# Loading x of the next block in eight transfers, each behind its own weight fetch, in a linear-attention and gated feed-forward kernel

## The chip, the core and the metric

One core of a Trainium2 chip runs the whole program. The metric is the device time of one execution in microseconds (us). Five engines work side by side, each through its own queue in order: TensorE (PE in the profile, its weight loads PEld), VectorE (DVE), ScalarE (ACT), GpSimd (POOL) and SyncE (SP), which issues nearly all transfers (DMAs) here. An instruction that waits holds up everything behind it in its engine's queue.

## The reference

Linear attention over 8 batches, 8 heads, 576 tokens and a head width of 64, followed by a feed-forward stage in which two products are multiplied element by element:

```python
def phi(x):
    proj = np.einsum('bhsd,df->bhsf', x, w_phi)
    proj = proj - np.max(np.abs(proj), axis=-1, keepdims=True)
    return np.concatenate([np.exp(proj), np.exp(-proj)], axis=-1)
q_p, k_p = (phi(q), phi(k))
kv = np.einsum('bhsf,bhsd->bhfd', k_p, v)
z = np.sum(k_p, axis=2)
num = np.einsum('bhsf,bhfd->bhsd', q_p, kv)
den = np.einsum('bhsf,bhf->bhs', q_p, z)[..., None] + 1e-06
attn = num / den                      # 8 x 8 x 576 x 64
x = attn.transpose(0, 2, 1, 3)        # 4608 tokens x 512
a = x @ w_a                           # 512 x 1536
b = x @ w_b
out = (a * b) @ w_out                 # 1536 x 512
```

The weights of the second stage are 64-bit floats, which the kernel decodes itself. All products are made in single precision out of two parts: each operand is split into a high part that TensorE takes and the low remainder, and three matmuls (high by high, low by high, high by low) stand for one.

## The kernel before

**The two passes.** The attention leaves x, normalised, in device memory, one buffer `xnorm[b]` for each batch of 576 tokens. The feed-forward stage runs over its 1536 inner columns in two halves. The first pass makes the first 768 columns, in blocks of 384 tokens, between the steps of the attention, and leaves its partial result in `part`. The second pass (`second_pass`, L803) makes the other 768 columns in six blocks of 768 tokens and adds `part`. This is the stretch from about 804.6 us to the end.

**A block of the second pass.** It works on three "quads" q = 0, 1, 2, each two columns of 128 wide, by Winograd's form of a 2 by 2 block product with seven factors: w11, w12, s2, s1, s3, w22, s4. One product (`product`, L721) multiplies one factor of the weights a and b by the same factor of x, in 12 matmuls of 128 by 128 by 384 columns: 21 products, 252 matmuls in a block. `evict` copies a product from PSUM with ScalarE, `add` adds the next one with VectorE, and `hi` and `lo` split the results h. The products with the output weights (L843, 126 matmuls in a block) follow, partly between those of the third quad.

**The streamed weights.** The factors of a and b lie in device memory (`kept`). Every product ends with `feed()` (L1016), which fetches (`fetch`, L566) the factor of the fourth product after it, 512 KB, into the slot that the product has just set free; a ring of four slots. So a fetch waits at the head of SyncE's queue until its product's matmuls are done, and has to land before the fourth product after it. Counted through a block, the feeds are: 1 to 5 for quad 0 (w11 to s3), 6 and 7 for quad 1 (w11, w12), 8 and 9 for quad 0 (w22, s4), 10 to 12 for quad 1 (s2, s1, s3), 13 and 14 for quad 2 (w11, w12), 15 and 16 for quad 1 (w22, s4), 17 and 18 for quad 2 (s2, s1), 19 to 21 for the rest of quad 2.

**x of the next block.** `factors_of_x(j + 1)` (L658) is a generator that `second_pass` moves on between its own steps. It fills two tiles `x32` of 128 partitions by 2 halves by 768 tokens, c = 0 and c = 1. A block of 768 tokens always spans two batches, so each tile takes two loads, and each load brings both halves i = 0 and 1 of the model's 512 rows for one run of tokens. After the four loads come the factors of x: for each factor and c a cast to the high part by ScalarE and a subtraction by VectorE (L156 and L163 in `split`), with four more subtractions for each c (L690 to L693).

**The order.** The kernel's instructions are put into the engines' queues by a planner, which goes by the program's order as priority and by its own estimate of when each operand is ready. `behind(feeds, ...)` (L392) ties a transfer's place in SyncE's queue to a place after the last fetch that has been made so far. The four loads of a block are tied to feeds 9, 11, 12 and 14. The three first loads of `part` (`given_load`, L817) are tied to feed 16. For the first block (j = 0) the loads are issued without such a tie, at the end of the first pass; there the tiles `x32` are shared with the decoding of the weights.

Of the kernel before, what the change touches and what calls it, by code (L numbers as in the profile page):

```python
# [3 lines left out]

# [14 lines left out]
P = 128  # L19
# [43 lines left out]
def tile_kernel(ctx, tc, qP, qD, km, kr, vm, vr, w_phi, w_two, eye, w_a, w_b, w_out, out):  # L63
# [13 lines left out]
    nc = tc.nc  # L77
    B, H, _, S = qD.shape
# [23 lines left out]
    xnorm = [dpool.tile([DM, S], F32, name=f"xnorm{b}") for b in range(B)]  # L102
# [57 lines left out]
    def split(hi, lo, src, eng_hi, eng_lo):  # L160

        copy(eng_hi, hi, src)
        eng_lo.tensor_tensor(lo, src, hi, op=ALU.subtract)  # L163
# [228 lines left out]
    def behind(what, issue):  # L392

        with tc.issue_after(what[-1].ins):
            issue()
# [170 lines left out]
    def fetch(key, place, name):  # L566
        t = place[0].tile([P, 2, 2, DM // 2], F32R, tag=place[1], name=f"back_{name}")
        feeds.append(nc.sync.dma_start(t.bitcast(F32), kept[key]))
        weights[key] = t
# [88 lines left out]
    def factors_of_x(j, pool, xs):  # L658


        n = T2 // 2
        half = NCC // 2
        x = [None] * NCC
        for c in range(half):
            x32 = pool.tile([P, 2, T2], F32, tag="x32", bufs=2, name=f"x32_1_{j}_{c}")
            x[c], x[c + half] = x32[:, 0], x32[:, 1]
            t = j * T2
            while t < (j + 1) * T2:
                b, s0 = divmod(t, S)
                m, t0 = min(S - s0, (j + 1) * T2 - t), t - j * T2  # L670
                rows = xnorm[b].rearrange("(i c p) s -> p c i s", i=2, p=P)[:, c, :, s0 : s0 + m]
                load = lambda: (nc.sync if j else nc.sync).dma_start(x32[:, :, t0 : t0 + m], rows)
                behind(feeds, load) if j else load()
                t += m
                yield

        def factor(c, k, src):
            hl = [pool.tile([P, n], F32R, tag=f"x{k}{part}", bufs=half, name=f"x{k}{part}_1_{j}_{c}") for part in "hl"]
            split(*hl, src, nc.scalar, nc.vector)
            xs[c][k] = hl  # L680

        for k, i in (("w11", 0), ("w12", half)):
            for c in range(half):
                factor(c, k, x[c + i][:, :n])
                yield
        for c in range(half):
            (x11, x12), (x21, x22) = ((t[:, :n], t[:, n:]) for t in (x[c], x[c + half]))
            sums = pool.tile([P, 2, n], F32, tag="xs", name=f"xs_1_{j}_{c}")
            t1, t2, t3, t4 = sums[:, 0], sums[:, 1], x12, x21
            nc.vector.tensor_tensor(t1, x12, x11, op=ALU.subtract)  # L690
            nc.vector.tensor_tensor(t2, x22, t1, op=ALU.subtract)
            nc.vector.tensor_tensor(t3, x22, x12, op=ALU.subtract)
            nc.vector.tensor_tensor(t4, x21, t2, op=ALU.subtract)  # L693
            yield
            factor(c, "s2", t2)
            factor(c, "s1", t1)
            yield
            factor(c, "s3", t3)
            factor(c, "w22", t4)
            yield  # L700
        for c in range(half):
            factor(c, "s4", x[c + half][:, n:])
            yield
# [3 lines left out]
    def in_turn(issue, wanted):  # L707
        with tc.issue_after(issued[0].ins) if issued[0] and wanted else nullcontext():
            issued[0] = issue()

    def winograd(q, xs, hs, u, spaces, feed):


# [7 lines left out]
        def product(k, to):  # L721
            start = to not in acc
            if start:
                opened(to)
            for i, nm in enumerate("ab"):
                w = weight(q, nm, k)
                for c in range(NCC // 2):
                    xh, xl = xs[c][k]
                    cols = slice(c * P, (c + 1) * P)
                    for n_, (w_, x_) in enumerate(((w[:, 0, cols], xh), (w[:, 0, cols], xl), (w[:, 1, cols], xh))):  # L730
                        at = dict(start=(start and c == n_ == 0), stop=(c > 0 and n_ == 2))
                        in_turn(lambda: nc.tensor.matmul(acc[to][i], w_, x_, skip_group_check=True, **at), u.startswith("1_0"))  # L732
            feed()
# [67 lines left out]
        yield  # L801

    def second_pass(xs, spaces, feed):  # L803
        n = T2 // 2
        pool = pools_moe[-1]
        nq = NFS[1] // 2
        for j in range(NT // T2):
            src, dst = (t.rearrange("(c p) s -> p c s", p=P)[:, :, j * T2 : (j + 1) * T2] for t in (part, out))
            hs = [{} for _ in range(nq)]
            x_next = factors_of_x(j + 1, spaces["x"], xs) if (j + 1) * T2 < NT else iter(())  # L810
            quads = [winograd(q, xs, hs[q], f"1_{j}_{q}", spaces, feed) for q in range(nq)]
            acc, given, us = {}, {}, []
# [107 lines left out]
    def run(work, steps=None):  # L920

        while work and steps != 0:
            if next(work[0], work) is work:
                work.popleft()
            elif steps is not None:
                steps -= 1
# [8 lines left out]
    def home(f, nm):  # L935
        return wpool, f"w_{f}_{nm}"

    kept, begun, feeds = {}, set(), []
    weights, pools_moe, xpools, block_x, blocks, marks, loads = {}, [ps_moe], [xpool], {}, [0], [], []
    with ExitStack() as c:  # L940
        pools = attention_pools(c)
# [39 lines left out]
    with ExitStack() as c:  # L981
        pool = c.enter_context(tc.tile_pool(name="stage", bufs=1))
        stage = stage_second(xin, pool)
        ahead = itertools.chain(
            *(load_factors(q, nm, stage, own, pool) for q in range(nq) for nm in "ab"),
            factors_of_x(0, xin, xs),
        )
        last = work.pop()
        due = 0.0
        while work:  # L990
            run(work, 1)
            due += AHEAD
            while due >= 1:
                next(ahead, None)
                due -= 1
        for _ in ahead:
            pass
        next(last)
        outs = deque(pair for pair in pairs if pair[0] == "o")
        places = deque()  # L1000
        for f in range(NFS[0]):
            next(last)
            for nm in "ab":
                if outs:
                    own[outs.popleft()] = home(f, nm)
                else:
                    places.append(home(f, nm))
            if f % 2:
                for _ in load_factors(f // 2, "o", stage, own, pool):
                    pass  # L1010
# [5 lines left out]
    def feed():  # L1016

        used[0] += 1
        if used[0] > FIRST and order:
            key = order.popleft()  # L1020
            fetch(key, ring[0], "_".join(map(str, (used[0], *key))))
            ring.rotate(-1)

    run(deque([last]))
    places.extend(home(f, "o") for f in range(NFS[0]))
# [67 lines left out]
```

## Time and profile before

| | |
|---|---|
| runs | 1215.03, 1215.25 and 1224.24 us, median 1215.25 us |
| profiled execution | 1216.38 us, with a span of 1214.6 us from first to last instruction |
| granted TensorE clock | 0.999 of full speed over the span |
| PE busy | 1180.6 us, 97% |
| DVE busy | 972.5 us, 80% |
| ACT busy | 778.3 us, 64% |
| device memory traffic | 225.14 MB, mean 185 GB/s |

A row of the profile names the line of the kernel, the engine, the operation, the tile written and the tiles read ("pa<-xw11h,back_w": the product of a, from the high part of x's factor w11 and a fetched weight tile). In brackets stands how long the engine was idle before the instruction and what released it. PE's busy time includes pipelined overlap, so its lost time shows better at the weight loads, of which one stands before each matmul.

### The profile page before, as it was taken

The page shows a single profiled execution, that of the slowest core. Times are in us where ns is not written, and L with a number is a line of the kernel's source. Part 1 is how long each engine was busy: PE and PEld are TensorE (multiplying, and loading weights), DVE is VectorE, ACT ScalarE, POOL GpSimd, SP SyncE. Part 2 cuts the span into 40 slices and gives each one's busy share as a digit, 9 for nine tenths or more (in the row PEclk, how much of TensorE's full clock was granted, in tenths as well). Part 3 has the DMA queues.
Part 4 walks back from the last instruction along what each step waited for, and adds up shares of the span by engine and source line. Part 5 has one row for each costly group of instructions (what it writes and reads, how often), then busy time and mean ns, then how long its engine had stood idle before and what let it go on. Part 6 is the DMA issues. An engine that isn't in the chain of part 4 may idle for free.

```text
span 1214.6 us, 20190 instructions
## 1 busy us (share of the span) xinstructions
PE 1180.6 (97%) x7086; PEld 1124.5 (93%) x7086; DVE 972.5 (80%) x1733; ACT 778.3 (64%) x1656; POOL 152.4 (13%) x69
## 2 busy tenths in 40 slices
PE   8889999999999999999999999999999999999998
PEld 5567788999999999999999999999999999999997
DVE  6967888988898989898888478977768596868665
ACT  5767788878888878888788445644435353535332
POOL 2322222121221121131122000000000000000000
PEclk9999999999999999999999999999999999999999
DMA  8766764554455454545342578759586776768572
GB/s 234 225 213 183 190 185 120 151 157 124 143 146 152 129 155 114 160 128 174 109 132 55 161 241 296 258 161 317 170 270 214 224 249 216 258 202 298 169 245 86
DMA packets 146166, 225.14 MB, mean 185 GB/s; under 512 B 40912, under 2 KB 87760, under 8 KB 146064
## 3 DMA queue, kind: packets, MB, share of 16 engines
q1 hardware_dynamic: 145616, 223.58, 60.7%
q8 instruction: 56, 0.92, 0.3%
q14 instruction: 46, 0.38, 0.1%
q10 hardware_dynamic: 448, 0.26, 0.1%
HBM read 174.74 MB, written 49.05 MB: 184 GB/s over the span
## 4 chain that ended last, share of the span: by engine, by line
PE 58%; DVE 18%; DMA 14%; ACT 5%; issue 3%; SPq 1%; DVEq 0%; ACTq 0%
PE po L843 9%; PE pa L732 8%; PE pb L732 8%; PE pa L619 6%; PE po L642 6%; PE pb L619 6%; PE kvps L304 6%; PE pn L386 5%; DMA x<-xnorm 3%; PE pq L362 2%; PE pk L247 1%; DMA part<-o 1%; DVE qs L168 1%; DMA rec<-r 1%; DMA raw_a<-in_w_a 1%
## 5 line engine op out<-in xcount | busy, mean ns | idle before, releaser
L366 POOL PARTITION_ALL_REDUCE mb<-p x64 | 152.1, 2377 | 523.3 <-ACT p L363 441.9
L619 PE MATMUL pa<-xh,w_a 128*128 128x384 f32 x576 | 166.2, 341 | 2.4 <-ACT kvh L329 1.2
L619 PE MATMUL pb<-xh,w_b 128*128 128x384 f32 x576 | 161.4, 338 | 0.0
L642 PE MATMUL po<-hh,w_o 128*128 128x384 f32 x576 | 153.0, 338 | 1.8 <-ACT hh L156 1.2
L619 PEld LDWEIGHTS pa<-xh,w_a 128*128 128x128 f32 x576 | 105.3, 188 | 4.2 <-ACT kvh L329 1.6
L642 PEld LDWEIGHTS po<-hh,w_o 128*128 128x128 f32 x576 | 104.0, 188 | 3.1 <-ACT hh L156 1.5
L619 PEld LDWEIGHTS pb<-xh,w_b 128*128 128x128 f32 x576 | 104.8, 188 | 0.5
L642 PE MATMUL po<-hl,w_o 128*128 128x384 f32 x288 | 96.7, 338 | 1.1 <-DVE hl L163 1.1
L619 PE MATMUL pa<-xl,w_a 128*128 128x384 f32 x288 | 97.7, 339 | 0.0
L619 PE MATMUL pb<-xl,w_b 128*128 128x384 f32 x288 | 96.7, 336 | 0.0
L163 DVE TENSOR_TENSOR qel<-qe,qeh 128x1152 fp32r<-128x1152 f32 x46 | 62.3, 1354 | 30.0 <-ACT qeh L156 26.6
L843 PE MATMUL po<-hh_s,own_o 128*128 128x384 f32 x288 | 80.3, 336 | 0.7 <-ACT u L831 0.5
L168 DVE TENSOR_TENSOR qs<-q,qs 64x576 fp32r<-64x576 f32 x52 | 64.1, 1232 | 14.6 <-ACT qs L156 13.4
L843 PE MATMUL po<-hh_w,own_o 128*128 128x384 f32 x216 | 59.1, 334 | 0.0
L387 ACT COPY xn<-pn 65x288 f32<-65x288 f32 x128 | 49.1, 396 | 15.3 <-PE pn L386 12.9
L261 ACT ACTIVATE ke<-kd 128x512 f32<-128x512 f32 x64 | 40.8, 638 | 24.5 <-DVE kd L253 22.3
L642 PEld LDWEIGHTS po<-hl,w_o 128*128 128x128 f32 x288 | 54.1, 188 | 1.9 <-DVE hl L163 1.7
L156 ACT CAST qeh<-qe 128x1152 fp32r<-128x1152 f32 x46 | 53.4, 1161 | 2.3 <-PE pn L386 2.2
L370 ACT ACTIVATE qe<-p 128x576 f32<-128x576 f32 x64 | 44.6, 696 | 15.7 <-DVE qel L163 10.5
L843 PEld LDWEIGHTS po<-hh_s,own_o 128*128 128x128 f32 x288 | 52.6, 188 | 2.0 <-ACT u L831 1.2
L619 PEld LDWEIGHTS pa<-xl,w_a 128*128 128x128 f32 x288 | 54.2, 188 | 0.3
L619 PEld LDWEIGHTS pb<-xl,w_b 128*128 128x128 f32 x288 | 54.1, 188 | 0.1
(302 smaller groups left out, 3421.4 us busy)
## 6 DMA issues: line engine op xcount, KB each, us to landing
back_s<-kept_s SPq DMA_DIRECT2D x71, 512.0 KB
back_w<-kept_w SPq DMA_DIRECT2D x52, 512.0 KB
q<-in_qD SPq DMA_DIRECT2D x52, 288.0 KB
k<-in_km SPq DMA_DIRECT2D x55, 256.0 KB
xun<-xn SPq DMA_DIRECT2D x64, 144.0 KB
x<-xun SPq DMA_DIRECT2D x32, 288.0 KB
rb<-rec SPq DMA_DIRECT2D x32, 288.0 KB
xnorm<-x SPq DMA_DIRECT2D x32, 288.0 KB
```

The lines of the kernel that those rows point to most:

```text
L156: eng.copy(dst, src)
L163: eng_lo.tensor_tensor(lo, src, hi, op=ALU.subtract)
L168: eng_lo.tensor_tensor(hi_lo[D:], src[D:], hi_lo[D:], op=ALU.subtract)
L304: nc.tensor.matmul(st["kv_ps", b, pr][:width, j], v_[:, j, :width], e_[:, j], start=(left == NFULL and j == 0 and n_ == 0), stop=(left == ...
L366: nc.gpsimd.partition_all_reduce(mb, p32, P, bass_isa.ReduceOp.absmax)
L370: nc.scalar.activation(e[:, 0], p32, AF.Exp)
L386: nc.tensor.matmul(pn[: D + 1, :HALF], kv_[:, 2 * j + s, :], e_[:, s, tok], **at)
L387: nc.scalar.copy(xn[: D + 1, tok], pn[: D + 1, :HALF])
L619: nc.tensor.matmul(acc, w[:, cc * P : (cc + 1) * P], x, start=(k == 0), stop=(k == 3 * NCC - 1))
L642: nc.tensor.matmul(accs[cc], w[:, cc * P : (cc + 1) * P], h, **at)
L732: in_turn(lambda: nc.tensor.matmul(acc[to][i], w_, x_, skip_group_check=True, **at), u.startswith("1_0"))
L843: in_turn(lambda: nc.tensor.matmul(acc[m, to], w_, h_, skip_group_check=True, **f), False)
```

## The change

`factors_of_x` makes two loads out of each: one for i = 0 and one for i = 1, so eight loads of half the size (288, 192 or 96 KB for 576, 384 or 192 KB). All eight are made when the generator is first moved on; for j > 0 they are not issued there but put into a queue, `between`. `feed()` takes one of them off after each fetch and places it behind that fetch. The generator still gives way four times before the factors, so its later steps fall where they fell; whatever is left in the queue by then is issued at once. The first move comes after feed 9, so the eight loads stand behind feeds 10 to 17. For j = 0 all eight are issued at the first step, with no tie.

```diff
+from functools import partial
...
                 m, t0 = min(S - s0, (j + 1) * T2 - t), t - j * T2
-                rows = xnorm[b].rearrange("(i c p) s -> p c i s", i=2, p=P)[:, c, :, s0 : s0 + m]
-                load = lambda: (nc.sync if j else nc.sync).dma_start(x32[:, :, t0 : t0 + m], rows)
-                behind(feeds, load) if j else load()
+                for i in range(2):
+                    rows = xnorm[b].rearrange("(i c p) s -> p c i s", i=2, p=P)[:, c, i, s0 : s0 + m]
+                    load = partial(nc.sync.dma_start, x32[:, i, t0 : t0 + m], rows)
+                    between.append(load) if j else load()
                 t += m
-                yield
+        for _ in range(4):
+            yield
+        while between:
+            behind(feeds, between.popleft())
...
-    kept, begun, feeds = {}, set(), []
+    kept, begun, feeds, between = {}, set(), [], deque()
...
             fetch(key, ring[0], "_".join(map(str, (used[0], *key))))
             ring.rotate(-1)
+            if between:
+                behind(feeds, between.popleft())
```

## Rows read from the trace of the kernel before

**Rows 1.** The page's first part, busy time and share of the span by engine.

```profile
PE 1180.6 (97%) x7086; PEld 1124.5 (93%) x7086; DVE 972.5 (80%) x1733; ACT 778.3 (64%) x1656; POOL 152.4 (13%) x69
```

**Rows 2.** Busy time in one stretch, the first five blocks of the second pass. Columns: the stretch and its length, PE, PEld, DVE, ACT and POOL busy with instruction counts, granted clock, DMA share, GB/s.

```profile
804.60:1141.00 336.40, 330.47 (x1887) 326.77 (x1888) 249.37 (x502) 145.05 (x318) 0.00 (x0) 1.00 0.72 234
```

**Rows 3.** The chain of work that ended last, in order of time: start, length, what. One run of six matmuls without a stall.

```profile
971.80 1.04 PE pa L732 x6
```

**Rows 4.** Who waited for whom from 804 to 1193 us: who, for what, us in total, times, longest. Weight loads (PEld) only.

```profile
PEld pa L732 <- ACT top L740: 5.0, 7, 1.3
PEld pa L732 <- ACT hh_w L748: 1.9, 1, 1.9
PEld pa L732 <- ACT low L740: 1.6, 2, 0.8
...
PEld pb L732 <- ACT low L740: 1.1, 1, 1.1
```

**Rows 5.** The timeline of PE and of its weight loads at single waits: start, length, engine, line, what, and in brackets the idle time before it and its releaser.

```profile
916.84 0.19 PEld L732 LDWEIGHTS pa<-xs3h,back_s 128*128 128x128 f32 x1 [0.31 <-ACT top L740]
...
965.29 0.41 PE L732 MATMUL pa<-xw11h,back_w 128*128 128x384 f32 x1 [1.65 <-DMA back_w<-kept_w]
...
1097.56 0.19 PEld L732 LDWEIGHTS pa<-xw11h,back_w 128*128 128x128 f32 x1 [0.73 <-ACT top L740]
...
1117.87 0.19 PEld L732 LDWEIGHTS pa<-xs3h,back_s 128*128 128x128 f32 x1 [0.57 <-ACT top L740]
...
1165.30 0.19 PEld L732 LDWEIGHTS pa<-xw11h,back_w 128*128 128x128 f32 x1 [0.96 <-ACT top L740]
```

**Rows 6.** SyncE's timeline in the third block of the pass (with one load of the second block ahead): start, time until the last issue of the row ended, what, count. Here the fetch of feed 9 is at 959.51, feeds 10 and 11 at 961.59, 13 and 12 (the planner has them in this order) at 967.67, 14 at 971.83, 15 and 17 at 973.91, 16 at 978.07.

```profile
901.77 0.43 SPq L672 DMA_DIRECT2D x<-xnorm  x1
...
959.51 0.32 SPq L568 DMA_DIRECT2D back_w<-kept_w  x1
959.93 0.39 SPq L672 DMA_DIRECT2D x<-xnorm  x1
961.59 2.40 SPq L568 DMA_DIRECT2D back_w<-kept_w  x2
964.05 0.44 SPq L672 DMA_DIRECT2D x<-xnorm  x1
967.67 2.40 SPq L568 DMA_DIRECT2D back_s<-kept_s  x2
970.13 0.43 SPq L672 DMA_DIRECT2D x<-xnorm  x1
971.83 0.32 SPq L568 DMA_DIRECT2D back_s<-kept_s  x1
972.21 0.43 SPq L672 DMA_DIRECT2D x<-xnorm  x1
973.91 2.40 SPq L568 DMA_DIRECT2D back_s<-kept_s  x2
978.07 0.32 SPq L568 DMA_DIRECT2D back_w<-kept_w  x1
978.44 2.63 SPq L821 DMA_DIRECT2D o<-part  x3
```

**Rows 7.** The chain that ended last, in order of time: single transfers from their issue to the release of what waited for them. The first is a load of x, the second a fetch of 512 KB, the third a store of 192 KB, the fourth a load of 384 KB.

```profile
896.10 6.97 DMA x<-xnorm
...
959.51 5.65 DMA back_w<-kept_w
...
1198.85 1.94 DMA out_x<-o
...
1200.84 3.50 DMA o<-part
```

**Rows 8.** ScalarE's timeline in the second block (first two rows) and the third.

```profile
903.15 0.51 ACT L156 CAST xw11h<-x 128x384 fp32r<-128x384 f32 x1 [3.51 <-DMA x<-xnorm]
903.57 0.47 ACT L740 COPY low<-pb 128x384 f32<-128x384 f32 x1
...
976.67 0.51 ACT L156 CAST xw11h<-x 128x384 fp32r<-128x384 f32 x1 [2.90 <-DMA x<-xnorm]
```

**Rows 9.** Busy time by stretch in the third block; columns as in rows 2.

```profile
974.00:979.00 5.00, 5.00 (x31) 5.00 (x30) 3.29 (x8) 2.17 (x5) 0.00 (x0) 1.00 1.01 368
...
984.00:989.00 5.00, 5.00 (x31) 5.00 (x30) 5.00 (x12) 4.29 (x11) 0.00 (x0) 1.00 0.58 197
989.00:994.00 5.00, 5.00 (x30) 5.00 (x29) 5.00 (x12) 3.29 (x8) 0.00 (x0) 1.00 0.48 152
...
999.00:1007.00 8.00, 8.00 (x48) 8.00 (x47) 5.49 (x12) 4.09 (x9) 0.00 (x0) 1.00 0.66 191
```

**Rows 10.** The timelines of PE and VectorE: the first matmul of the block after, which reads the new x, and the first subtraction on the tile c = 1.

```profile
993.48 0.33 PE L732 MATMUL pa<-xw11h,back_w 128*128 128x384 f32 x1
...
977.22 0.56 DVE L163 TENSOR_TENSOR xw11l<-x,xw11h 128x384 fp32r<-128x384 f32 x1 [1.71 <-ACT xw11h L156]
```

**Rows 11.** SyncE's own waits over the second pass, and one issue of a transfer of 128 rows (a store) in its timeline.

```profile
SPq L568 <- PE pb L732: 198.5, 100, 9.6
...
874.08 0.34 SPq L828 DMA_DIRECT2D out_x<-o  x1
```

**Rows 12.** Busy time in the stretch between the attention's end and the second pass; columns as in rows 2.

```profile
757.00:804.60 47.60, 46.42 (x268) 46.09 (x266) 46.53 (x111) 29.95 (x72) 0.00 (x0) 1.00 0.69 226
```

## The prediction

> **What bounds the kernel now.** I read the page's first part, then the busy time of the five blocks that load a next x, then the waits of TensorE's weight loads, and last the queues around the x loads. TensorE is busy 97% of the span [rows 1], so only a stall of TensorE can be won. How much there is to win comes from a count. A block has 252 + 126 = 378 matmuls, and an undisturbed run takes 1.04 us for six [rows 3], so a block without a stall takes 65.5 us and five take 327.6. They took 336.4 [rows 2]: 8.8 us are lost in five blocks, 0.7% of the whole time. That is the ceiling of anything done to x's loads in this pass.
>
> Where the lost time sits: the weight loads waited 5.0 us for ScalarE's evictions "top", 2.7 us for "low" (1.6 and 1.1), and 1.9 us for what the view calls a cast [rows 4]. That last one is really a fetch: the matmul at 965.29 was released by the landing of `back_w` after 1.65 us [rows 5], and the fetch, of feed 9, took 5.65 us from its issue to that release [rows 7]. The waits for "low" of 1.1 us stand behind x: at 903.15 ScalarE had sat 3.51 us before a cast of x, and the eviction comes right behind it in the same queue [rows 8].
>
> **The change, part by part.**
>
> *The load behind feed 9 goes.* Now an x load is issued 0.4 us after that fetch (959.93 after 959.51), and the product that needs the fetch would have started at 965.29 - 1.65 = 963.64, 4.1 us after its issue [rows 5, 6]. The first part will stand behind feed 10, so this fetch runs with nothing of x after it for two more microseconds. The wait cannot fall to zero: the last block loads no x, and there the same place waits 0.96 us for "top" [rows 5]. What is late next is thus that eviction. Of the third block's wait of 1.9 us [rows 4] I count 1.9 - 0.5 = 1.4 gained, of the fifth block's 0.73 [rows 5] 0.2, with 0.5 as the remainder, between nothing and the 0.96. Sum: 1.6 us gained. Ends: no gain, and 1.9 + 0.7 = 2.6.
>
> *x arrives later.* The first tile (c = 0) is complete now with the second load. Afterwards its last part stands behind feed 12, which the planner has put after 13: in the second block that is the place of the load at 901.77 [rows 6]. A load of x took 976.67 - 972.21 = 4.5 us [rows 6, 8] to 7.0 us [rows 7] to the release of its cast, so c = 0 would be ready at about 906.3 to 908.8 instead of 903.1, that is 3.1 to 5.6 us later. The second tile's last part moves behind feeds 16 and 17, to about 978.4 from 972.21, 6.2 us later [rows 6]. Its landing then lies near 983, still 10 us before the first matmul that reads it at 993.48 [rows 10]. Two subtractions on it (0.56 us each, the first at 977.22 [rows 10]) move into a stretch where VectorE is full, 5.00 of 5.00 us at 984 and at 989; after 999 it has 2.5 us free out of 8 [rows 9]. Price between 0 and 1.1 us a block, 5.5 in all; I take 0, because PE has no idle time in those rows and the new x has the 10 us.
>
> *Where ScalarE then waits.* The casts of x stand among the evictions of quads 1 and 2, and the planner places them by its own estimate of the landing. If the casts move back with the loads, the stall of 1.1 us at 904 goes and those of 0.31 and 0.57 us for "top" and 1.6 us for "low" [rows 4, 5], at the evictions of quad 2, may grow, since more of x's work now falls beside them. Ends: all of these gone, -(1.1 + 0.3 + 0.6 + 1.6) = -3.6 us; or the casts stay ahead of the evictions, and the 3.1 us is paid in each of five blocks, +15.5. I take 0: the planner knows that the parts are tied to later fetches, and moves their casts; what it does not know, the landing under load, it has wrong by as much now as then.
>
> *More transfers, the same bytes.* Four more issues a block, 0.34 us each by the store of 128 rows, are 1.4 us of SyncE; it waits 198.5 us for PE in front of fetches [rows 11]. That wait is the cover. Without it each part would hold the next fetch by 0.3 us. I take 0. The load rate flattens: x is spread over eight products where it stood in six. In the densest row the DMA engines were busy throughout, at 368 GB/s [rows 9], so the bytes that move out of such a stretch free it, but what waits on fetches there has slack: PE runs 5.00 of 5.00.
>
> *The first block.* Its eight loads are issued up to three steps earlier in the program's order, with no tie. PE loses 1.2 of 47.6 us there [rows 12], so nothing large is to be won; four issues more are 1.4 us of SyncE ahead of weight loads that PE's work covers. I take 0, with ends -0.5 and +1.4.
>
> **Sum.** 1216.38 us for the profiled execution, less 1.6, is 1214.8. That execution stands 1.1 above the median of the runs shown, 1215.25, so on the median's scale: 1213.6 us.
>
> **A rule that speaks against it.** A 192 KB store took 1.94 us and a 384 KB load 3.50 [rows 7], so 192 KB more cost 1.56 us; of the smaller transfer 1.94 - 1.56 = 0.38 us is then a fixed part, an estimate across two kinds of transfer. The Trainium skill (DMA: Bandwidth & Descriptors, Rules for kernel authors) says to merge small transfers into one large one and names 1 MiB for full bandwidth, which would forbid the halving. The rows agree in sign, not in weight, for the parts here. By the rule the time would be that of the third rival; by the rows it is the sum above.
>
> **Rivals.**
> 1. *All of x's stalls go*: fetch 9 at its full gain (2.6) and the evictions' 3.6 us give 1215.25 - 6.2 = 1209.0; with every loss of these blocks gone, 8.8, 1206.4. For it: the DMA engines are full exactly where x comes. Against it: the place after feed 9 waits for "top" in the block without x too.
> 2. *ScalarE's queue holds an eviction behind a later x* (slower). Place: the copy "low" behind the cast of c = 0 [rows 8]. Price: 3.1 us in each block where the planner leaves the cast ahead of the copy. It decides from the point where c = 0 lands later than the copy could run. In two blocks it gives 1213.6 + 6.2 = 1219.8, in all five 1229.1. For it: x is later by design, and ScalarE has waited 3.51 us for this landing already [rows 8]. Against it: the planned place moves too.
> 3. *Each transfer has its fixed price in a full queue*: four times 0.38 is 1.5 us of delay a block for fetches at feeds 10 to 17. If no slack took it up, 7.6 us in five blocks, 1222.9. Against it: those fetches have four products' time, some 8 us, before they are needed.
> 4. *The change does nothing*: the planner puts the parts into the same order of landing, or gains and losses cancel: 1215.3.
>
> **How the numbers follow.** Chances: forecast 0.58, its own range 1210.5 to 1217; rival 1 0.13; rival 2 0.16, a third of it in all blocks; rival 3 0.04; rival 4 0.09. About 1% is what a measurement of this kernel can tell from no change: below 1203.1 or above 1227.4. No case reaches 1203; I leave 0.02 for a new order by the planner that nobody asked for. Slower by over 1% is the hard form of rival 2 with something for rival 3 and for a bad order: 0.07. The rest, 0.91, is within 1%. The range leaves out the hard form of rival 2 and the ends: from 1207.5, between rival 1's two values, to 1221, over rival 2's soft form.
>
> **What would show it.** Right: x loads of the later pass alternate with fetches, 40 instead of 20, each of 288, 192 or 96 KB; the wait of the third block's first w11 product of quad 2 falls from 1.9 to about 0.5 us with "top" as its releaser; the five blocks together take 333 to 336 us. For rival 1 they take 330 or less, with hardly a PE wait for "low". For rival 2 ScalarE sits longer in front of `xw11h` and PE right behind it for "low". For rival 3 the fetches of feeds 10 to 17 take longer from issue to release, and PE waits for `back_s`. My forecast is wrong if the five blocks change by more than 6 us, or if the first pass or its end, before 804.6 us, moves by more than 2 us.

## The result, and the profile after

The changed kernel took 1236.43 us in the median of six executions (1229.49 to 1237.91), the kernel before 1217.97 us beside them: a ratio of 1.0121, with a 95% interval of 1.0091 to 1.0151. (Every ratio here is an estimate from all executions of both kernels; the two medians alone would give 1.0152.) The prediction had 1213.6 us, no higher than 1221, and 91% on a change of less than 1%.

The profiled execution of after took 1229.49 us, the shortest of the six, with a span of 1227.7 us; it is 13.1 us above the one of before, so the loss in this trace is smaller than that of the medians, 18.5 us. The first part of its page, to be held against [rows 1]:

```profile
PE 1184.6 (96%) x7086; PEld 1127.0 (92%) x7086; DVE 973.5 (79%) x1733; ACT 779.9 (64%) x1656; POOL 152.8 (12%) x69
```

The counts are the same: no engine has more to do, yet PE is busy 4.0 us longer and idle for the other 9.1. Windows tell where. First the second pass of the kernel before, from its first matmul (columns as in rows 2):

```profile
804.65:1214.00 409.35, 398.17 (x2268) 392.57 (x2268) 291.88 (x583) 166.31 (x363) 0.00 (x0) 1.00 0.68 222
```

Then the same matmuls of after, and below them its first five blocks (1887 matmuls, as in [rows 2]) and three short stretches:

```profile
806.97:1154.40 347.43, 335.06 (x1887) 329.44 (x1888) 250.29 (x502) 146.07 (x318) 0.00 (x0) 0.99 0.70 227
806.97:1227.00 420.03, 402.82 (x2268) 395.34 (x2268) 292.85 (x583) 167.35 (x363) 0.00 (x0) 0.99 0.67 216
808.30:811.50 3.20, 3.20 (x12) 3.20 (x12) 2.52 (x7) 1.42 (x4) 0.00 (x0) 0.50 0.82 294
922.60:925.80 3.20, 2.37 (x12) 2.05 (x12) 3.20 (x8) 2.56 (x7) 0.00 (x0) 1.00 0.12 47
1060.80:1064.00 3.20, 3.20 (x10) 3.20 (x11) 3.19 (x7) 1.18 (x4) 0.00 (x0) 0.51 0.24 95
```

The pass begins 2.3 us later and takes 10.7 us more. The prediction had allowed 2 us for that start, but the 2.3 need not come from the change: two kernels further down (e6, e12) have the instructions of before in the same order on every engine up to here, and their passes begin at 808.21 and 799.78. Of the 10.7 us, 6.0 are idle time of PE (420.03 - 402.82 = 17.2 for 409.35 - 398.17 = 11.2), and for 4.7 PE is busy longer. Two stretches of 3.2 us at about half the granted clock account for some 3.2 of these. The loss lies in the five blocks that load a next x, which took 347.4 us for 336.4; the prediction had called itself wrong from a change of 6 us on. Who waited for whom in the second pass of after, from 804 to 1206 us (columns as in [rows 4]):

```profile
ACT xw12h L157 <- DMA x<-xnorm: 14.7, 7, 3.9
ACT xw11h L157 <- DMA x<-xnorm: 12.7, 8, 3.6
PEld pa L737 <- ACT top L745: 12.6, 9, 3.1
...
PEld pa L737 <- ACT low L745: 3.9, 4, 1.3
```

And in the same view of before, ScalarE's wait for x:

```profile
ACT xw11h L156 <- DMA x<-xnorm: 13.3, 7, 3.5
```

ScalarE waits 27.4 us for x where it waited 13.3, and PE's weight loads wait 12.6 us for "top", for 5.0 before [rows 4]. The timeline of PE at the longest of these waits, and that of PE or its weight loads at the two places where before had waited for a fetch:

```profile
922.60 0.44 PE L737 MATMUL pa<-xs3h,back_s 128*128 128x384 f32 x1 [2.56 <-ACT top L745]
...
970.42 0.19 PEld L737 LDWEIGHTS pa<-xw11h,back_w 128*128 128x128 f32 x1 [0.84 <-ACT top L745]
970.45 0.41 PE L737 MATMUL pa<-xw11h,back_w 128*128 128x384 f32 x1 [0.55 <-ACT top L745]
...
991.26 0.44 PE L737 MATMUL pa<-xs3h,back_s 128*128 128x384 f32 x1 [0.80 <-ACT top L745]
...
1060.75 0.59 PE L737 MATMUL pa<-xs3h,back_s 128*128 128x384 f32 x1 [2.76 <-ACT top L745]
...
1109.04 0.19 PEld L737 LDWEIGHTS pa<-xw11h,back_w 128*128 128x128 f32 x1 [0.53 <-ACT top L745]
...
1130.78 0.44 PE L737 MATMUL pa<-xs3h,back_s 128*128 128x384 f32 x1 [1.71 <-ACT top L745]
```

The rows at 970.4 and 1109.04 are the third and fifth block's first product of quad 2: the predicted gain came (1.65 us for a fetch in [rows 5] became 0.55 for "top"). The other four rows are one place, the product s3 of quad 2, in four of the five blocks. In before the weight load at the same place waited 0.31 us in the second block and 0.57 in the fifth [rows 5]. What stands behind it is told by the chain of waits in the second block (start, length, what):

```profile
914.19 6.21 DMA x<-xnorm
...
920.42 0.51 ACT xw11h L157
920.94 0.15 ACT hh_s L753
...
921.25 0.51 ACT xs1h L157
921.76 0.41 ACT hh_s L753
922.17 0.38 ACT top L745
...
922.60 1.32 PE pa L737 x6
```

Read from the bottom: PE waits for the eviction "top", which stands in ScalarE's queue behind two splits `hh_s` of quad 1 and casts of x, and the first of those casts waits for the last part of x, issued at 914.19. In the third, fourth and fifth block the chain to the same place also passes through VectorE, where a subtraction on x (L695) stands ahead of quad 1's last step (L796); the clearest case of that stands under e2.

ScalarE's timeline in the second block of after has the waits in brackets:

```profile
911.70 0.51 ACT L157 CAST xw11h<-x 128x384 fp32r<-128x384 f32 x1 [1.05 <-DMA x<-xnorm]
...
916.78 0.51 ACT L157 CAST xw12h<-x 128x384 fp32r<-128x384 f32 x1 [1.63 <-DMA x<-xnorm]
...
918.15 0.51 ACT L753 CAST hh_s<-top 128x384 fp32r<-128x384 f32 x1 [0.45 <-DVE top L792]
920.42 0.51 ACT L157 CAST xw11h<-x 128x384 fp32r<-128x384 f32 x1 [1.76 <-DMA x<-xnorm]
920.84 0.51 ACT L753 CAST hh_s<-low 128x384 fp32r<-128x384 f32 x1
...
922.08 0.47 ACT L745 COPY top<-pa 128x384 f32<-128x384 f32 x1
```

In before the casts of the second tile stood just as much ahead of quad 1's splits, and x was there in time:

```profile
910.29 0.51 ACT L156 CAST xw11h<-x 128x384 fp32r<-128x384 f32 x1 [1.33 <-DMA x<-xnorm]
910.71 0.51 ACT L156 CAST xw12h<-x 128x384 fp32r<-128x384 f32 x1
...
913.55 0.52 ACT L748 CAST hh_s<-top 128x384 fp32r<-128x384 f32 x1 [0.67 <-DVE top L787]
...
916.31 0.47 ACT L740 COPY top<-pa 128x384 f32<-128x384 f32 x1
```

The loads moved back; the casts of the second tile hardly did: of them only `xw11h` moved, behind one of three splits. Those of the first tile did move: in this block they now stand, from 908.05 on, behind quad 1's copy "low" at 905.41, as the prediction had it, and the wait of 1.1 us for that copy [rows 4, 8] is gone.

How late x is shows in the cast `xw11h` of each tile, which in both kernels starts when x lands: 911.70 for 903.15 [rows 8] with c = 0, 920.42 for 910.29 with c = 1. The block itself is 4.0 us later by then, as VectorE's first addition of "low" shows, in before and in after:

```profile
899.67 0.56 DVE L744 TENSOR_TENSOR low<-pa,low 128x384 f32<-128x384 f32 x1 [2.43 <-ACT low L740]
```

```profile
903.67 0.56 DVE L749 TENSOR_TENSOR low<-pa,low 128x384 f32<-128x384 f32 x1 [2.46 <-ACT low L745]
```

Against its own block, x is 8.5 - 4.0 = 4.5 us later with c = 0 and 10.1 - 4.0 = 6.1 with c = 1.

### The profile page after: what moved, and what is told of

It is laid out like the page before. It is cut to its first block, busy times and chain, and to the rows that moved or that the text cites. A ratio compares the mean times of both kernels' runs of the same rounds, so it can differ in the third digit from the quotient of the medians.

```text
span 1227.7 us, 20239 instructions
## 1 busy us (share of the span) xinstructions
PE 1184.6 (96%) x7086; PEld 1127.0 (92%) x7086; DVE 973.5 (79%) x1733; ACT 779.9 (64%) x1656; POOL 152.8 (12%) x69
## 4 chain that ended last, share of the span: by engine, by line
PE 52%; DVE 19%; DMA 16%; ACT 7%; issue 4%; SPq 1%; DVEq 0%; ACTq 0%
PE pa L737 9%; PE pb L737 9%; PE po L848 8%; PE pa L620 6%; PE pb L620 6%; DMA x<-xnorm 5%; PE kvps L305 5%; PE po L643 4%; PE pn L387 4%; DMA rec<-r 2%; DVE qs L169 2%; PE pq L363 1%; DMA rb<-rec 1%; DMA raw_a<-in_w_a 1%; PE pk L248 1%
```

## The experiments

Two theories stood at the start. **A**: the places of the loads cost, because x lands later and ScalarE's queue, with the casts of x in it, holds the evictions. **B** (rival 3): the number of transfers costs. A ratio is to the kernel before, run beside it on the same chip, with its 95% interval.

**Eight halves at the old places (e1).** Against before, each load is cut in two, still behind feeds 9, 11, 12 and 14:

```diff
-                load = lambda: (nc.sync if j else nc.sync).dma_start(x32[:, :, t0 : t0 + m], rows)
-                behind(feeds, load) if j else load()
+                for i in range(2):
...
+                    load = partial(nc.sync.dma_start, x32[:, i, t0 : t0 + m], rows)
+                    behind(feeds, load) if j else load()
```

> Edit: the eight half loads of the change, but two of them behind each of the fetches where the four whole loads stood (feeds 9, 11, 12, 14); the first block's loads halved too, two at each step. Theory A (the later places of the parts are what costs: the casts of tile c = 1 wait in ScalarE's queue ahead of the casts and the eviction 'top' that quad 2's s3 product needs): ratio to before 0.997 to 1.004, PE's waits for 'top' back to about 5 us. Theory B (eight transfers of half the size cost more than four): ratio 1.009 to 1.013, as the change itself. Theory C (the first block's loads at the first step, and the slower start after 804 us that follows, cost the time): ratio 1.000 to 1.004, with the start of the pass as before.

1.0005 [0.9990, 1.0020]. Eight transfers for four, and four more issues a block, cost nothing that can be measured here (the weight loads' wait for "top" is 6.3 us, for 5.0 in before). B falls. The Trainium skill (DMA: Bandwidth & Descriptors, Rules for kernel authors) says to join small transfers into large ones; for parts of 288, 192 and 96 KB beside this much other traffic the run shows no price.

**Four whole loads at late places (e2).** Against before, uncut, behind feeds 11, 13, 15 and 17:

```diff
-                behind(feeds, load) if j else load()
+                between.extend((None, load)) if j else load()
...
+            load = between.popleft() if between else None
+            if load:
+                behind(feeds, load)
```

> Edit: four whole loads as before, but late: behind feeds 11, 13, 15 and 17, so that each tile is complete where the change completes it; the first block as before. Theory A: ratio to before 1.007 to 1.014, ScalarE waits 2 to 4 us per block for x in front of the casts of quad 1's h, and PE waits 2 to 3 us at quad 2's s3 for 'top'. Theory B: 0.998 to 1.003. Theory C: 0.998 to 1.003.

1.0116 [1.0082, 1.0149]: the whole loss without any halving. Two waits of its second pass, and PE's timeline at the longest of them, in the fourth block, show the same place as after:

```profile
ACT xw11h L157 <- DMA x<-xnorm: 25.4, 10, 4.3
PEld pa L737 <- ACT top L745: 11.8, 10, 4.4
```

```profile
1060.80 0.69 PE L737 MATMUL pa<-xs3h,back_s 128*128 128x384 f32 x1 [4.09 <-ACT top L745]
```

But here the chain of waits that leads to it goes through VectorE:

```profile
1047.75 5.77 DMA x<-xnorm
...
1053.64 0.56 DVE xs L695
...
1057.95 0.47 DVE x L698
1058.42 0.47 DVE low L793
...
1059.36 0.48 DVE low L796
...
1059.86 0.51 ACT hh_s L753
1060.37 0.39 ACT top L745
```

From the landing of x on, VectorE worked without a pause. Eight of its instructions (L695 to L698 and four subtractions of `split`), at 0.47 us each 3.8 us in all, are for the next x and stand in its queue ahead of L796, the step that quad 1's last split needs, and "top" stands behind that split in ScalarE's queue. So theory A holds with VectorE's queue beside ScalarE's.

**The change without its part for the first block (e3).** The loads for j = 0 go back to four, one at each step:

```diff
-                    between.append(load) if j else load()
+                if j:
...
+                else:
+                    rows = xnorm[b].rearrange("(i c p) s -> p c i s", i=2, p=P)[:, c, :, s0 : s0 + m]
+                    nc.sync.dma_start(x32[:, :, t0 : t0 + m], rows)
```

> Edit: the change, with the first block's four loads whole and one at each step as before. Theory A: ratio to before 1.008 to 1.012; the wait at the start of the pass goes back from 2.5 to about 1.4 us and its stretch at the lower clock goes, 2 to 3 us in all. Theory B: 1.010 to 1.013. Theory C: 0.998 to 1.004.

1.0096 [1.0062, 1.0129]. The five blocks carry at least most of the loss; whether the first block's loads carry the remaining 0.25% is not told apart, since the two intervals overlap. The traces leave little for them: PE's wait at the first matmul of the pass is 1.1 to 2.0 us in the kernels with the first block's loads of before (nine profiles, this one at 1.1), and 2.0 to 2.7 us in the four that issue all eight at the first step.

**The change, with casts moved in ScalarE's queue (e4).** The splits of the second tile (c = 1), that is its casts and the subtractions that need them, are placed behind quad 2's "top", so that its casts cannot stand ahead of it:

```diff
-            split(*hl, src, nc.scalar, nc.vector)
+            with tc.issue_after(held[0].ins) if j and c else nullcontext():
+                split(*hl, src, nc.scalar, nc.vector)
...
-        evict(top1, 0)
+        held[0] = evict(top1, 0)
```

> Edit: the change, with the seven ScalarE casts of tile c = 1 of the next x placed in ScalarE's queue behind quad 2's first eviction 'top'; all transfers stand as in the change. Theory A: PE's wait at quad 2's s3 falls from 2 to 3 us to under 1 us in each block, and the ratio to before falls to 0.999 to 1.005. If VectorE's subtractions on the late tile hold the chain instead of the casts, the wait stays and the ratio is 1.008 or more. Theory B: 1.010 to 1.013. Theory C: 1.010 to 1.013.

1.0045 [1.0023, 1.0067]. With the loads of the change untouched, the place of one tile's splits takes 0.76 of the 1.21%. The weight load in front of the same product in the second block, for which after waited till 922.60:

```profile
917.98 0.19 PEld L738 LDWEIGHTS pa<-xs3h,back_s 128*128 128x128 f32 x1 [0.55 <-ACT top L746]
```

The queues, then, and not the landing by itself: no matmul waited for x in either kernel. Since casts and subtractions move together here, the run does not tell ScalarE's share from VectorE's. The other 0.45% was not followed further; in this trace PE waits 4.7 us for fetches, where before had 2.1 and after 0.5, and its weight loads still wait 7.2 us for "top".

**One tile late at a time (e6, e7).** Whole loads again, each behind a feed that a table names. First the second tile alone:

```diff
-                behind(feeds, load) if j else load()
+                held_back.append(load) if j else load()
...
+            at = {9: 0, 11: 1, 15: 2, 17: 3}
+            if 9 in at:
+                behind(feeds, held_back[at[9]])
+            between.extend(held_back[at[n]] if n in at else None for n in range(10, max(at) + 1))
```

> Edit: four whole loads, tile c = 0 as before (feeds 9 and 11), tile c = 1 late (feeds 15 and 17). If the lateness of c = 1 alone makes the loss: ratio to before 1.007 to 1.012, PE waiting 2 to 4 us at quad 2's s3 for 'top'. If c = 0 makes it: 0.998 to 1.003. If both share: 1.003 to 1.007.

1.0022 [1.0001, 1.0043]. Then the first tile alone; the second keeps the feeds that it has in before, 12 and 14:

```diff
-            at = {9: 0, 11: 1, 15: 2, 17: 3}
+            at = {11: 0, 13: 1, 12: 2, 14: 3}
```

> Edit: four whole loads, tile c = 0 late (feeds 11 and 13), tile c = 1 about as before (feeds 12 and 14). If the lateness of c = 1 makes the loss: ratio to before 0.998 to 1.004. If that of c = 0 does (the place that the prediction's second rival named, the eviction 'low' of quad 1 behind the cast of c = 0): 1.007 to 1.012 with PE's waits for 'low' grown by 1 us or more in a block.

1.0046 [1.0025, 1.0068]. I had looked for nearly the whole loss in the second tile, whose cast ends the chain shown above. Both tiles count, and 0.22 + 0.46 = 0.68% is less than the 1.16% with both late (e2), though the intervals are wide enough that the gap may be much smaller. Why the two together cost more was not settled.

**Eight parts at early places (e5).** The generator is moved on after feed 5 in place of feed 9, so the parts stand behind feeds 6 to 13:

```diff
+                if q == 0:
+                    next(x_next, None)
...
-                if q == 0:
-                    next(x_next, None)
```

> Edit: the change with the generator's first step made after feed 5 instead of feed 9, so that the same eight parts stand behind feeds 6 to 13 and x is complete one product earlier than before the change; the factor steps stay where they were. Theory A (late landing of tile c = 1 holds ScalarE's queue): ratio to before 0.993 to 1.001, with ScalarE's waits for x under half of the 27 us of the change and no wait of PE over 1 us for 'top' in the blocks. Theory B (eight halves, each behind a fetch of its own, delay the fetches): 1.004 to 1.012 still, since as many transfers stand between the fetches.

1.0015 [0.9995, 1.0035]. ScalarE's waits for x nearly went, and PE waited for fetches in their place. One wait of its second pass, and the first of its three cases in PE's timeline:

```profile
PE pa L737 <- DMA back_w<-kept_w: 4.9, 3, 1.8
```

```profile
905.24 0.41 PE L737 MATMUL pa<-xw11h,back_w 128*128 128x384 f32 x1 [1.49 <-DMA back_w<-kept_w]
```

In this trace an x that comes earlier is paid for in fetches, at the very product (first of quad 2) where before had its longest wait for a fetch [rows 5]. And one wait for "top" of nearly 3 us came against the expectation, in the first block, at the product s3 of quad 1. There the subtraction on x stood in VectorE's queue ahead of quad 0's last steps, and waited for x:

```profile
831.64 0.56 DVE L695 TENSOR_TENSOR xs<-x 128x384 f32<-128x384 f32 x1 [2.36 <-DMA x<-xnorm]
```

```profile
835.25 0.69 PE L737 MATMUL pa<-xs3h,back_s 128*128 128x384 f32 x1 [2.99 <-ACT top L745]
```

VectorE's queue can thus hold "top" with no cast of x in the chain.

**Can x's work stand later?** Before's loads, with the splits of c = 0 behind quad 1's "low" and those of c = 1 behind quad 2's "top" (e8):

```diff
-            split(*hl, src, nc.scalar, nc.vector)
+            with tc.issue_after(held[c].ins) if j else nullcontext():
+                split(*hl, src, nc.scalar, nc.vector)
...
+        if q == NFS[1] // 2 - 1:
+            held[1] = top
...
+        if q == 1:
+            held[0] = low_
```

> Edit: the kernel before, transfers unchanged, with the casts of tile c = 0 placed in ScalarE's queue behind the eviction 'low' of quad 1 and those of c = 1 behind the eviction 'top' of quad 2. Theory A, that casts of x ahead of evictions are what costs PE time, also for the kernel before: ratio 0.994 to 0.999 (2 to 6 us of the 8.8 us that its five blocks lose). If its remaining waits are fetches and the planner's order: 0.999 to 1.003.

0.9987 [0.9964, 1.0011], not told from before. Next all of x's work, casts and subtractions of both tiles, behind quad 1's last cast and its last subtraction; first with the loads of the change (e10), then with those of before (e11):

```diff
-            split(*hl, src, nc.scalar, nc.vector)
+            with after_chain(j):
+                split(*hl, src, nc.scalar, nc.vector)
...
+        if q == 1:
+            held[:] = chain_end
```

> Edit: the change's transfers untouched, but all work on the next x, ScalarE's casts and VectorE's subtractions on both tiles, is placed in its engine's queue behind the last cast and the last subtraction of quad 1's h (factor w22). Theory A in its full form (x's work in the two in-order queues, ahead of quad 1's chain of h, is the whole cost of the late transfers): ratio to before 0.997 to 1.003, against 1.0121 for the change and 1.0045 with the casts of c = 1 alone moved; PE's waits for 'top' at most as before. If the late fetches behind the parts hold the rest: 1.003 to 1.006 with PE waiting 4 us or more for back_w and back_s. If the x work, now later, is missing in front of the next block: over 1.006, with PE waiting at the next block's w11.

> Edit: the kernel before with its own four loads, all work on the next x placed behind quad 1's chain in the same way. Theory A: 0.994 to 0.999, since the stalls for 'top' and 'low' that stood beside x in the kernel before (3.6 us) go. If moving the work back costs as much as it frees: 0.999 to 1.003.

1.0098 [1.0078, 1.0117] and 1.0091 [1.0072, 1.0110]: the loads no longer matter, and both lose nearly as much as the change. The weight loads' waits for "top" went back to 4.7 and 4.8 us, and new waits stand in the output stage, not at the next block's w11, which the expectation had named. The weight loads of the third block, in the first of the two:

```profile
1003.83 0.19 PEld L746 LDWEIGHTS pa<-xw12h,back_w 128*128 128x128 f32 x1 [1.21 <-DVE o L841]
1006.71 0.30 PEld L859 LDWEIGHTS po<-hh_s,own_o 128*128 128x128 f32 x2 [0.82 <-ACT hh_s L762]
1007.57 0.19 PEld L859 LDWEIGHTS po<-hl_s,own_o 128*128 128x128 f32 x1 [0.56 <-DVE hl_s L765]
1008.98 0.19 PEld L859 LDWEIGHTS po<-hl_s,own_o 128*128 128x128 f32 x1 [0.40 <-DVE hl_s L765]
1010.21 0.19 PEld L859 LDWEIGHTS po<-hh_s,own_o 128*128 128x128 f32 x1 [0.59 <-ACT u L847]
```

That is 3.6 us in one block. I had expected before's loads to lose little in this form. The two tiles' work together finds no free place behind quad 1's chain, neither on ScalarE nor on VectorE, for both of which PE waits here.

**The predicted gain alone (e12).** Whole loads, the first moved from behind feed 9 to behind feed 10, the others where before has them. The same table as in e6:

```diff
-            at = {9: 0, 11: 1, 15: 2, 17: 3}
+            at = {10: 0, 11: 1, 12: 2, 14: 3}
```

> Edit: four whole loads, the first behind feed 10 instead of feed 9, the others where they were (11, 12, 14). It does alone what the prediction's one gain rests on, the fetch of feed 9 with no x behind it. By the prediction's step: the wait of the third block at quad 2's first w11 falls from 1.9 to about 0.5 us, ratio 0.997 to 1.000. If that fetch is late for other reasons (the last block waits there too): the wait stays and the ratio is 0.999 to 1.003.

0.9974 [0.9956, 0.9991]: 1215.89 us for 1218.81, the lowest ratio of all these kernels, and ahead of both that the study began with. The weight load of the third block's first product of quad 2:

```profile
958.73 0.19 PEld L742 LDWEIGHTS pa<-xw11h,back_w 128*128 128x128 f32 x1 [0.54 <-ACT top L750]
```

The wait fell from 1.94 to 0.54 us, as expected. That this is what gained the 0.26% is not shown. The profiled execution is 5.2 us shorter than the one of before, but 4.9 us of that lie ahead of the pass (it begins at 799.78 for 804.65), where both kernels have the same instructions in the same order; from its first matmul to its last the pass takes 405.8 us for 406.1. In the fourth block a wait of 0.75 us is new, for the fetch that now has the load of x behind it (w12 of quad 2).

**That, with x's work placed as in e8 (e13).** The edit of e8 on top of e12:

> Edit: the kernel before with its four whole loads behind feeds 10, 11, 12 and 14, and the casts of tile c = 0 behind quad 1's eviction 'low', those of c = 1 behind quad 2's eviction 'top'. If the freed fetch (ratio 0.9974 alone) and the freed evictions (0.9987 alone, not told from 1) are separate stalls, they add: 0.994 to 0.998. If they are the same slack twice: 0.997 to 1.000.

0.9981 [0.9967, 0.9995]. Nothing was added that can be told from e12.

## Why the prediction was wrong

- **The gain at feed 9**: right. I counted 1.4 and 0.2 us for the third and fifth block. In after, the weight load's wait at the third went from 1.94 to 0.84 us and at the fifth from 0.73 to 0.53, 1.3 us in all, with "top" next, as said. With this alone (e12) the medians differ by 2.9 us (1218.81 - 1215.89), just above the upper end of 2.6 that I gave; the interval of the ratio is 1.1 to 5.4 us, and the trace does not show that all of it comes from this fetch.
- **x arrives later**: the lateness was right (3.1 to 5.6 us forecast for c = 0, 4.5 measured; 6.2 forecast for the last load of c = 1, 6.1 measured). Its price of 0 failed. I had judged it by the reader of x, ten microseconds later, and by PE's full rows. No matmul waited for x. What paid was other work in the same queues.
- **"I take 0: the planner knows that the parts are tied to later fetches, and moves their casts"**: this is the step that failed. The planner did move the first tile's casts behind "low" in the second block. But the work on the second tile kept its place ahead of quad 1's last splits, the casts in ScalarE's queue and the subtractions in VectorE's. While it waited for x, those splits waited too, and then "top": the weight loads' wait for "top" went from 5.0 to 12.6 us. Taking one tile's splits out of the way gave back 0.76 of 1.21% (e4). The upper end that I had worked out for this term, +15.5 us, is near the measured loss (14.7 us by the ratio, 18.5 by the medians), but I had priced it at another place, so that is partly chance.
- **Rival 2** was the mechanism, at another place. I had put it at the copy "low" behind the cast of c = 0, 3.1 us in each block. The weight loads' wait for "low", both products together, grew only from 2.7 to 3.9 us, that for "top" from 5.0 to 12.6. The stall is later: x's work, quad 1's splits, quad 2's "top". Its hard form (1229.1 us) lay above my range, because I held it unlikely in all five blocks. It came in four of them at s3.
- **VectorE**, where I had put the moved subtractions at 0, was the other half of the same mistake: I had looked at how full its stretch is and not at what stands behind x's work in its queue. In e2's longest stall that is 3.8 us of x's work ahead of quad 1's last step. Nor is the place behind quad 1's chain free: with all of x's work moved there both kernels lose 0.9 to 1.0% (e10, e11).
- **More transfers at 0** and **the first block at about 0**: the first is borne out by e1, so rival 3 falls; the second stays open within 0.25% (e3), and the waits at the start of the pass speak for about 1 us.
- **Rivals 1 and 4** fell: ScalarE's stalls grew, and the kernel did not stay the same. The ceiling of 8.8 us on any gain held.
- **Not in the sum at all**: the granted clock. The two stretches at half clock cost the profiled execution some 3.2 us. The mean granted clock of after's six executions was 0.991, that of the 19 executions of before beside the first experiments 0.997, and that of e4's ten 0.998. As an estimate from these, the time lost to the clock is 0.009 x 1236 = 11 us in after against 0.003 x 1217 = 4 us in before, so some 7 us of the loss may be clock. How the rest divides was not measured.

## What to carry to other kernels

To move a load back, look not at the first matmul that reads it but at the first instructions that touch it, on every engine, and at what stands behind each of them in its engine's queue; if the order of those queues does not move with the load, the wait is paid by whatever is next there. Move one load at a time: here the kernel with the first one moved back by a single fetch was 0.26% faster, and the one with all of them moved back lost 1.21%. Before work is put off, see whether the stretch that it goes to is free on every engine that it uses.

## What the runs showed of the hardware

The granted clock fell in two places of the second pass of after. At 806.97 PE had been idle 2.29 us, started at full rate, and from 808.30 the clock was 0.50 for at least 3.2 us; at 1060.75 it had been idle 2.76 us, and the clock was 0.51 from there on, again for at least 3.2 us. After the 2.56 us before 922.60 it stayed at 1.00. In the run with late whole loads PE was idle 4.09 us before 1060.80, and the window of that run after it shows

```profile
1060.80:1067.20 6.40, 6.40 (x23) 6.40 (x24) 4.40 (x9) 3.88 (x10) 0.00 (x0) 0.60 0.16 47
```

so 6.4 us at 0.60, most of them at the lower of the two levels, 1.2 and 2.4 GHz. The Trainium skill (TensorE: Matmul & The Clock Gate, Part 1: The HAM clock gate) says that the array's clock goes by how busy it has been lately, half rate being the state without activity; these rows agree, and show that a stall of about 2.5 us sometimes brings it and sometimes does not. That the stalls cause the fall was not tried by itself; that e4, without the long stalls at s3, was granted 0.998 on average goes with it.
